# Attention with a compressed memory, then a mixture of experts: a new order of the instructions, gates stored apart, memory products in half-height tiles

## The chip, the cores and the metric

The kernel runs on one core of a Trainium2 chip. The metric is the device time of one execution in microseconds (us). Before the change the median of 3 runs is 526.75 us (526.15 to 527.25). Engines are named as in the profile: PE is TensorE (PEld its weight loads), DVE is VectorE, ACT is ScalarE, POOL is GpSimd, SP is SyncE, which starts most transfers.

## The reference, cut to what matters

Four batches with eight heads, 576 tokens and head size 64 go through causal attention. Beside it each query reads a memory, and a sigmoid of beta mixes the two. The mix, 2304 rows of 512, is routed to one of eight experts.

```python
scores = scale * np.matmul(q, k.transpose(0, 1, 3, 2))      # causal, softmax -> a
local = np.matmul(a, v)
q_p = phi(q)                                                # elu(q) + 1
mem_ret  = np.einsum('bhsd,bhde->bhse', q_p, M_prev)
mem_norm = np.einsum('bhsd,bhd->bhs', q_p, z_prev)[..., None] + 1e-06
x = g * (mem_ret / mem_norm) + (1 - g) * local              # [2304, 512]
logits = x @ w_gate; e_idx = np.argmax(logits, axis=1)
gate_w = softmax(logits)[e_idx]; eom = sigmoid(x @ w_output_gate)
for e in range(8):                                          # rows of expert e
    ye = np.maximum(x[mask] @ w1[e], 0) @ w2[e]
    out[mask] = gate_w[mask, None] * eom[mask, e, None] * ye
```

## The kernel before, in words

The kernel has three stages.

**Attention.** Work goes by pairs of heads, 16 pairs, four per batch. Per pair the scores are computed in query tiles of 128 rows (the last has 64), each fp32 operand split in a rounded part `hi` (C, ACT or DVE) and a rest `lo` (R, POOL). A score tile is masked and its row minimum taken on DVE (M, L555 and L523), turned to weights by ACT (E, L560 and L532), transposed on PE (T, L572 and L541), copied from PSUM by ACT or DVE (V, L419), and multiplied with the values (P, L607; O copies the result). `phi` of the queries is made by POOL, ACT and DVE (F0, F1, F2; L440, L444, L447). When a batch is done, per query tile the memory product (ME, L658), its norm and scaling (N1, N2), the local part turned back (PV, Y) and the sum (XD) follow, and the rows are written to a table `xs` in DRAM (OUT). The routing of a batch (RT, L225 to L239) finds the best expert of each row, RK ranks the rows by matmuls, Tgate and Tpos compute gate value and position on DVE, and SEL (L305, POOL) makes a selection matrix. For the last batch ME is followed by PL, YL, TL, XL and OL, in halves of heads. GO (L275) writes the gate values of a batch into column 512 of `xs`, whose rows are 513 wide.

The order of all this is not left to a scheduler. `ORDER` is a list of some 1150 job names in the file; the jobs are emitted in that order, and each engine runs its own in that order. A suffix (`:ACT`, `:DVE`) says which engine takes a job that two can do. The numbers in the `job(...)` calls (cost, due time, what is taken and used, `mode`, `port`) fed the planner that wrote the list; at run time they do nothing.

**Bridge.** After the list, the last batch is routed (`route`, `rank`, `tail_rank`), and slots of 128 rows are formed: `hit` matrices against the selection matrices give by matmuls (L977) the row number of each place in each slot. `warm(n)` issues n matmuls that nothing reads. Then the first rows are gathered from `xs` by indices (L1033, POOL).

**Experts.** 23 slots of 128 rows go through two matmuls each (L1083), weights split in `whi` and `wlo` as they arrive, and the scaled result is scattered to the output. The scale is the gate value, the 513th column of the gathered row.

The memory product before takes the two heads of a pair in one matmul over all 128 partitions against a block-diagonal matrix of 162 columns, half of them zeros:

```python
for hf in range(2):
    me = psm.tile([P, 324], F32, name=f"me{m}_{hf}", tag="m")
    for pp in range(2):
        T.matmul(me[:r, 162 * pp:162 * pp + 162], t["phi"][2 * hf + pp][:, qz], t["mz"][:, 2 * hf + pp, :], start=True, stop=True)
```

Of the kernel before, what the change touches and what calls it, by code (L numbers as in the profile page):

```python
# [49 lines left out]
SS2_1 F21 M2_0_0 M2_1_0 E2_0_0 F03 E2_1_0 C3:ACT T1_2_1 M2_0_1 V1_2_1:DVE T1_2_0 V1_2_0:DVE P0_256_1 F22 O0_256:ACT F13 M2_1_1 P1_0_0 T1_4 V1_4_0:DVE  # L50
R3 V1_4_1:DVE load4 SS1_3 E2_0_1 load5 M1_3_0 M1_3_1 E2_1_1 SS2_2 T2_0 T2_1 F04 C4:ACT V2_0:ACT MW1 load_v3 E1_3_1 M2_2_0 E2_2_0 gates E1_3_0 V2_1:DVE
SS2_4 T1_3_1 T2_2_0 M2_2_1 V2_2_0:ACT M2_4_0 TS1_0 SS2_3 V1_3_1:DVE M2_4_1 E2_2_1 O1_0:ACT T1_3_0 F05 T2_2_1 M2_3_1 M2_3_0 E2_4 R4 SS3_1 V1_3_0:ACT
E2_3_1 gates2 V2_2_1:DVE E2_3_0 SS3_2 M3_0_0 MC1 P1_256_0 F23 M3_0_1 M3_1_0 T2_3_1 F14 E3_0_0 T2_3_0 P1_256_1 V2_3_0:ACT E3_0_1 O1_256:ACT E3_1_0
V2_3_1:DVE C5:DVE T2_4 M3_1_1 V2_4_0:ACT ME0_0 T3_0 E3_1_1 M3_2_0 F15 V2_4_1:ACT SS3_4 TS1_1 V3_0:ACT M3_2_1 N10_0 SS4_1 TS2_0 T3_1 E3_2_0 N20_0 ME0_1
M3_4_0 R5 M4_0_0 M3_4_1 E3_2_1 M4_1_1 M4_1_0 V3_1:ACT E3_4 N10_1 T3_2_0 TS2_1 load6 M4_0_1 G0_0 T3_2_1 E4_1_1 E4_0_1 V3_2_0:ACT V3_2_1:DVE E4_0_0
SS3_3 N20_1 E4_1_0 SS4_2 F24 M3_3_0 T3_4 P2_256_0 E3_3_0 P2_0_0 V3_4_0:ACT P2_256_1 V3_4_1:ACT O2_256:ACT load_v4 T4_0 M3_3_1 C6:DVE O2_0:DVE TS3_1
T4_1 F25 V4_0:DVE M4_2_1 E3_3_1 ME0_4 M4_2_0 T3_3_0 V4_1:ACT N10_4 N20_4 E4_2_1 SS4_4 V3_3_0:ACT T4_2_1 V4_2_1:ACT E4_2_0 M4_4_0 T3_3_1 ME0_3 T4_2_0
# [1210 lines left out]
```

## Time and profile before

| What | us |
|---|---|
| median of 3 runs | 526.75 |
| profiled execution, device time | 526.39 |
| its span, first to last instruction | 524.4 |
| attention, to about 208.5 | 208.5 |
| bridge, to the first expert matmul | 17.5 |
| experts, to the end | 298.4 |
| PE busy, share of the span | 503.0, 96% |
| DVE, ACT, POOL busy | 340.9, 279.1, 291.1 |

The profiled execution lies 0.36 us below the median, and its device time 2.0 us above its span. A busy PE includes matmuls that wait in the pipeline: durations of single matmuls overlap, so the spacing of their starts is what they cost. PEclk 1.00 is the full clock (2.4 GHz), 0.50 half of it.

### The profile page before, as it was taken

To read this page: it belongs to the slowest core of one execution; us is meant where nothing else is said; L and a number is where in the kernel's file an instruction comes from. 1 tells how busy PE (TensorE), PEld (TensorE's weight loads), DVE (VectorE), ACT (ScalarE), POOL (GpSimd) and SP (SyncE) were. 2 spreads that over 40 slices of the span, in tenths; PEclk is the share of its full clock that TensorE was granted. 3 is DMA by queue.
4 is the path that set the end of the run, shared out by engine and by line. 5 is a ranking of instruction groups with operands and counts; after the bars stand their busy time and mean duration, and the time that the engine had idled before them with its cause. 6 is when DMAs were issued, how large, how long until landed. Compare 5 with 4: busy or idle time off the path is not lost.

```text
span 524.4 us, 10513 instructions
## 1 busy us (share of the span) xinstructions
PE 503.0 (96%) x3238; PEld 402.2 (77%) x3238; DVE 340.9 (65%) x821; ACT 279.1 (53%) x643; POOL 291.1 (56%) x264
## 2 busy tenths in 40 slices
PE   8999999999899999688999999999999999999994
PEld 4788778787777887366888888888888888888884
DVE  5998899999689988659898289500073891025600
ACT  5997788696677864353444333333444433343341
POOL 8882584676355223743577657644455675445342
PEclk9999999999699999889999999999999999999998
DMA  7632155263202513396777367511153675115000
GB/s 247 218 133 101 52 166 160 79 190 100 85 26 77 133 57 91 63 326 228 213 242 225 130 191 216 189 40 48 53 147 114 202 221 160 40 44 158 8 3 27
DMA packets 29079, 68.22 MB, mean 130 GB/s; under 512 B 6176, under 2 KB 6688, under 8 KB 29026
## 3 DMA queue, kind: packets, MB, share of 16 engines
q1 hardware_dynamic: 25186, 56.63, 35.3%
q0 software_dynamic: 3696, 10.77, 5.9%
q8 instruction: 32, 0.52, 0.4%
q14 instruction: 21, 0.17, 0.1%
q10 hardware_dynamic: 144, 0.13, 0.1%
HBM read 58.06 MB, written 10.76 MB: 131 GB/s over the span
## 4 chain that ended last, share of the span: by engine, by line
PE 84%; DVE 8%; POOL 3%; issue 3%; ACT 1%; POOLq 0%; DVEq 0%; ACTq 0%
PE h L1083 23%; PE py L1083 22%; PE pt L572 7%; PE po L607 7%; PE s L497 6%; PE me L658 4%; PE hp L1106 3%; PE sd L484 2%; DVE wlo L944 2%; PE px L1052 2%; PE pt L541 2%; PE pv L721 1%; POOL selp L305 1%; DVE st L555 1%; PE pl L824 1%
## 5 line engine op out<-in xcount | busy, mean ns | idle before, releaser
L941 DVE CAST whi<-raw 128x1024 fp32r<-128x1024 f32 x56 | 56.2, 1004 | 119.4 <-ACTq L1090 109.2
L1111 POOL TENSOR_TENSOR hl<-hT,hh 128x512 fp32r<-128x512 f32 x46 | 68.4, 1507 | 87.4 <-ACT hh L1110 87.4
L944 DVE TENSOR_TENSOR wlo<-raw,whi 128x1024 fp32r<-128x1024 f32 x63 | 95.0, 1508 | 4.0 <-ACT whi L941 1.1
L1083 PE MATMUL py<-whi,hh 128*128 (+1 forms) x192 | 77.8, 405 | 1.6 <-DVEq L947 1.6
L560 ACT ACTIVATE st<-st,nm 128x384 f32<-128x384 f32 (+3 forms) x128 | 71.2, 558 | 14.2 <-DVE nm L555 13.7
L1083 PE MATMUL py<-wlo,hh 128*128 (+1 forms) x192 | 74.2, 386 | 0.0
L1083 PE MATMUL py<-whi,hl 128*128 (+1 forms) x192 | 73.9, 385 | 0.0
L1083 PE MATMUL h<-whi,xh 128*128 (+1 forms) x184 | 73.9, 401 | 0.0
L1083 PE MATMUL h<-wlo,xh 128*128 (+1 forms) x184 | 73.0, 397 | 0.0
L1083 PE MATMUL h<-whi,xl 128*128 (+1 forms) x184 | 72.7, 395 | 0.0
L555 DVE CUSTOM_DVE_ANT_0 st<-s,mask 128x128 f32<-128x128 f32 (+3 forms) x128 | 57.9, 483 | 8.4 <-PE s L497 5.3
L1096 ACT ACTIVATE h<-h 128x1024 f32<-128x1024 f32 x23 | 23.6, 1026 | 73.4 <-PE h L1083 73.4
L392 POOL TENSOR_TENSOR lo<-qk,hi 128x1216 fp32r<-128x1216 f32 x15 | 43.1, 2870 | 27.7 <-ACT hi L388 21.3
L1110 ACT CAST hh<-hp 128x512 fp32r<-128x512 f32 x46 | 27.5, 598 | 48.7 <-PE py L1083 48.7
L419 ACT COPY PT<-pt 128x512 f32<-128x512 f32 (+2 forms) x84 | 42.1, 516 | 17.9 <-PE pt L572 14.5
L572 PE MATMUL pt<-ident,st 128*128 128x128 f32 x320 | 47.9, 281 | 3.2 <-ACT PT L419 2.4
L1060 POOL TENSOR_TENSOR xl<-x,xh 128x512 fp32r<-128x512 f32 x22 | 32.4, 1472 | 33.3 <-ACT x L1059 30.1
L1109 ACT COPY hT<-hp 128x512 f32<-128x512 f32 x46 | 27.2, 590 | 42.5 <-PE hp L1106 42.5
L607 PE MATMUL po<-PT,v 128*64 128x320 f32 (+4 forms) x480 | 47.8, 348 | 0.5 <-DVE oT L419 0.4
L572 PEld LDWEIGHTS pt<-ident,st 128*128 128x128 f32 x320 | 36.7, 143 | 9.7 <-ACT PT L419 4.1
L607 PEld LDWEIGHTS po<-PT,v 128*64 128x64 f32 x480 | 30.0, 137 | 18.4 <-issue 3.2
L1083 PEld LDWEIGHTS py<-whi,hh 128*128 128x128 f32 x192 | 36.2, 188 | 8.3 <-DVEq L947 2.2
(199 smaller groups left out, 998.6 us busy)
## 6 DMA issues: line engine op xcount, KB each, us to landing
raw<-in_w SPq DMA_DIRECT2D x64, 512.0 KB, 4.1
...
```

Of the source, the lines that this page charges most:

```text
L392: G.tensor_tensor(c["lo"][:, TQ:], c["raw"][:, TQ:], f32(c["hi"])[:, TQ:], op=ALU.subtract)
L419: (A.copy if e == "ACT" else V.tensor_copy)(dst(), src())
L497: T.matmul(c()["ss", q][j], l[r, lc], m[r, KC:KC + w], start=(a == 0), stop=(a == 2))
L555: V.tensor_tensor_reduce(st[:, :w], c()["ss", qt][j], mask[:, 512 - w:512], -SCALE, 3.0e38, ALU.add, ALU.min, negm()[:, i:i + 1])
L560: A.activation(st, st, AF.Exp, bias=c()["negm"][:, i:i + 1], scale=-1.0, accum_out=sums()[:, qt, 2 * p + j:2 * p + j + 1])
L572: T.transpose(pt[:, (m * k1 + i) * P:(m * k1 + i + 1) * P], st[:, i * P:(i + 1) * P], ident)
L607: T.matmul(po[64 * j:64 * j + 64, qs - q0:q1 - q0], vt[:, k, 64 * j:64 * j + 64], PT[:, j, k, qs:q1], start=(k == 0), stop=(k == kn - 1))
L941: join((A.copy if eng is A else eng.tensor_copy)(whi[:, e % 2, c, :], raws[e, c]))
L944: join(eng.tensor_tensor(wlo[:, e % 2, c, :], raws.pop((e, c)), f32(whi[:, e % 2, c, :]), op=ALU.subtract))
L1060: G.tensor_tensor(xl, x32, f32(xh), op=ALU.subtract)
L1083: i = T.matmul(o[n % nh], l[:, z], m[:, n * 512 + part.start:n * 512 + part.stop], start=(c == 0 and k == 0 and n < nh), stop=(c == 3 and ...
L1111: G.tensor_tensor(hl[:, z], hT[:, z], f32(hh)[:, z], op=ALU.subtract)
```

## The change

- `ORDER` is written anew for all engines. The jobs are the same but for those below; their order, and for V, O, LC and C the engine, differ. The first line of the list, as an example:

```diff
-first1 load2 SS0_1 M0_0_0 E0_0_0 M0_0_1 M0_1_1 E0_0_1 E0_1_1 first3 first2 M0_1_0 E0_1_0 F00 F01 SS0_3 SS0_2 M0_3_1 load_v2 T0_0 T0_1 M0_3_0 V0_0:DVE
+load2 SS0_1 first1 first2 M0_0_0 E0_0_0 M0_1_1 M0_1_0 M0_0_1 first3 E0_1_1 SS0_3 E0_0_1 M0_3_1 E0_1_0 C1:ACT M0_3_0 F00 SS0_2 T0_0 T0_1 SS0_4 E0_3_1
```

- Memory products: each head is a matmul of its own over 64 partitions and 81 columns, the two heads of a pair in the upper and the lower half of the array.

```diff
-            for hf in range(2):
-                me = psm.tile([P, 324], F32, name=f"me{m}_{hf}", tag="m")
-                for pp in range(2):
-                    T.matmul(me[:r, 162 * pp:162 * pp + 162], t["phi"][2 * hf + pp][:, qz], t["mz"][:, 2 * hf + pp, :], start=True, stop=True)
-                mes.append(me[:r].rearrange("p (h c) -> p h c", c=81))
+            me = [psm.tile([P, 324], F32, name=f"me{m}_{j}", tag="m") for j in range(2)]
+            for p in range(NP):
+                for j in range(2):
+                    z = slice(64 * j, 64 * j + 64)
+                    T.matmul(me[j][:, 81 * p:81 * p + 81], t["phi"][p][z, qz], t["mz"][z, p, 81 * j:81 * j + 81], start=True, stop=True)
+            mes.extend(x[:r].rearrange("p (h c) -> p h c", c=81) for x in me)
```

- Gates: the 128x5 gate values of a batch are transposed on PE (GP), copied from PSUM (GS, on DVE, on ACT for the last batch) into a buffer of which there is one, and written as 5 rows of 512 bytes to a table `gd` of their own (GO). `xs` rows are 512 wide. The expert stage gathers the gates of a slot with an indirect transfer of its own.

```diff
         def gate7():
-            SY.dma_start(xs[row(b, 0):row(b, NQ), DM:XW].rearrange("(t p) c -> p (t c)", p=P), t["og"])
+            t["gp"] = fin.get("pw", psm).tile([P, 512], F32, name=f"gp{b}", tag="m")
+            T.transpose(t["gp"][:NQ, :P], t["og"], ident)
+
+        def gate8():
+            t["gs"] = sm.tile([P, P], F32, name=f"gs{b}", tag="gs", bufs=1)
+            (A.copy if b == B - 1 else V.tensor_copy)(t["gs"][:NQ], t["gp"][:NQ, :P])
+
+        def gate9():
+            SY.dma_start(gd[row(b, 0):row(b, NQ)].rearrange("(t p) c -> t (p c)", p=P), t["gs"][:NQ])
...
+        job(f"GP{b}", "PE", 109, due + DUE["TG"], gate7, after=[before], takes=[("m", f"gp{b}")], uses=[("rb", b)], mode="F")
+        job(f"GS{b}", "DVE", 160, due + DUE["TG"], gate8, after=[f"GP{b}"] + ([f"GO{b - 1}"] if b else []), takes=[("gs", b)], uses=[("m", f"gp{b}")])
+        job(f"GO{b}", "SP", 400, due + DUE["TG"], gate9, after=[f"GS{b}"] + ([f"GO{b - 1}"] if b else []), uses=[("gs", b)], size=10)
...
+    def gather_gate(s):
+        g = st[s]["g"] = mk.tile([P, 1], F32, name=f"g{s}", tag="g", bufs=4)
+        G.indirect_dma_start(out=g, out_offset=None, in_=gd[:NT + 1], in_offset=bass.IndirectOffsetOnAxis(ap=rowi[:, s:s + 1], axis=0))
+
     def gather(s):
-        xr = mk.tile([P, XW], F32, name=f"xr{s}", tag="xr", bufs=4)
+        xr = mk.tile([P, DM], F32, name=f"xr{s}", tag="xr", bufs=4)
         G.indirect_dma_start(out=xr, out_offset=None, in_=xs[:NT + 1], in_offset=bass.IndirectOffsetOnAxis(ap=rowi[:, s:s + 1], axis=0))
         st[s] = {"x": xr, "ring": s < NMAIN}
+        if s > 2:
+            gather_gate(s)
...
-        A.activation(y, py, AF.Copy, scale=st[s]["x"][:, DM:DM + 1])
+        A.activation(y, py, AF.Copy, scale=st[s]["g"])
...
     low(0, 2)
     ready()
+    for s in range(3):
+        gather_gate(s)
```

- Bridge: the second `warm(11)` becomes `warm(22)`, and `warm` and GP take PSUM from a pool of their own there.

```diff
+    fin["pw"] = rx.enter_context(tc.tile_pool(name="pw", bufs=2, space=PSUM))
     warm(8)
...
-    warm(11)
+    warm(22)
```

Three places of the new order follow. The first is PE at the first memory product of batch 0 (`me0_0`; `pt` are transposes of weights, `sd` scores of the 64-row tile, `s` scores). Before:

```order
L541 MATMUL pt2_4_669<-ident_70,st2_4_567 128x128 x4
L543 MATMUL pte2_4_674<-ident_70,st2_4_567 64x128
L658 MATMUL me0_0_0_681<-mz0_184,phi0_223 128x162
L658 MATMUL me0_0_0_681<-mz0_184,phi1_225 128x162
L658 MATMUL me0_0_1_684<-mz0_184,phi2_397 128x162
L658 MATMUL me0_0_1_684<-mz0_184,phi3_448 128x162
L572 MATMUL pt3_0_0_687<-ident_70,st3_0_0_628 128x128
L572 MATMUL pt3_0_0_687<-ident_70,st3_0_1_639 128x128
```

And now:

```order
L508 MATMUL s3_2_0_670<-hi3_472 128x384
L508 MATMUL s3_2_1_671<-hi3_472 128x384
L670 MATMUL me0_0_0_680<-mz0_185,phi0_239 128x81
L670 MATMUL me0_0_1_681<-mz0_185,phi0_239 128x81
L670 MATMUL me0_0_0_680<-mz0_185,phi1_300 128x81
L670 MATMUL me0_0_1_681<-mz0_185,phi1_300 128x81
L670 MATMUL me0_0_0_680<-mz0_185,phi2_307 128x81
L670 MATMUL me0_0_1_681<-mz0_185,phi2_307 128x81
L670 MATMUL me0_0_0_680<-mz0_185,phi3_475 128x81
L670 MATMUL me0_0_1_681<-mz0_185,phi3_475 128x81
L495 MATMUL sd3_4_0_693<-lo3_473,hi3_472 128x288
L495 MATMUL sd3_4_0_693<-hi3_472,lo3_473 128x288
```

Four matmuls of 162 columns became eight of 81, with the two heads of a pair in turn. This product now stands behind row-tiled scores `s`, which read 64 partitions each as well; before it stood among matmuls over the whole array. Over the list, PE passes between layouts of its array (whole, two row halves, column tiles) 109 times now and 91 times before, counted by the jobs' modes.

The second is POOL in batch 1, around the rest of pair 13 (`lo13`; `selp` is a SEL of batch 0, `xd` an XD, `sums` copies of row sums). Before:

```order
L458 COPY sums2_1579<-sumd9_2018 64x1
L729 TENSOR_TENSOR xd1_4_2082<-x1_4_1442,y1_4_1983 64x512
L305 TENSOR_SCALAR selp_78<-pidx_74,pcol_76,tokv_73 128x128 x2
L392 TENSOR_TENSOR lo13_2085<-qk13_1563,hi13_2084 128x1216
L392 TENSOR_TENSOR lo14_2168<-qk14_2002,hi14_2167 128x1216
L458 COPY sums2_1579<-sumd10_2218 64x1
```

And now:

```order
L741 TENSOR_TENSOR xd1_4_2036<-x1_4_1451,y1_4_2019 64x512
L469 COPY sums2_1621<-sumd9_2095 64x1
L403 TENSOR_TENSOR lo13_2080<-qk13_1614,hi13_2079 128x1216
L469 COPY sums2_1621<-sumd8_1899 64x1
L469 COPY sums2_1621<-sumd10_2207 64x1
L316 TENSOR_SCALAR selp_79<-pidx_75,pcol_77,tokv_74 128x128 x2
```

The two SEL now stand behind `lo13`, and `lo14` no longer follows it. `lo14` now stands, behind a row sum of batch 3 (`sums3`) and another SEL:

```order
L469 COPY sums3_2476<-sumd12_2565 64x1
L316 TENSOR_SCALAR selp_79<-pidx_75,pcol_77,tokv_74 128x128
L403 TENSOR_TENSOR lo14_2396<-qk14_2082,hi14_2395 128x1216
L665 MEMSET lg3_2771 128x80
L403 TENSOR_TENSOR lo15_2803<-qk15_1810,hi15_2802 128x1216
L741 TENSOR_TENSOR xd2_2_2810<-x2_2_2496,y2_2_2706 128x512
```

There it is 17 rows of POOL later than before, next to `lo15`.

The third is DVE at the end of the list, from the last product of the last batch (`yl2_1`, job YLl2_1) to the routing of that batch (`mx3`). Before:

```order
L833 TENSOR_TENSOR yl2_1_3255<-pl2_1_3252,rr3_2896 128x320
L836 TENSOR_REDUCE lg3_2730<-yl3_1_3249 128x16
L836 TENSOR_REDUCE lg3_2730<-yl2_1_3255 128x16
L280 TENSOR_TENSOR pos2_3268<-rk2_3258,oha_77 128x40
L283 TENSOR_REDUCE ps2_3269<-pos2_3268 128x5
L286 TENSOR_SCALAR ohe_86<-ps2_3269 128x5
L289 TENSOR_TENSOR pcol_76<-ps2_3269,ohe_86 128x5
L811 CAST cntb_83<-cnt_82 128x8
L225 TENSOR_REDUCE mx3_3302<-lg3_2730 128x5
```

Now, its first seven rows and its last seven:

```order
L847 TENSOR_TENSOR yl2_1_3314<-pl2_1_3303,rr3_3032 128x320
L226 TENSOR_REDUCE mx2_3317<-lg2_1880 128x5
L230 TENSOR_TENSOR dl2_3319<-lg2_1880,mx2_3317 128x40
L234 SCALAR_TENSOR_TENSOR wt2_3321<-dl2_3319,edesc_80 128x40
L237 TENSOR_REDUCE mx2_3317<-wt2_3321 128x5
L240 SCALAR_TENSOR_TENSOR oha_78<-mx2_3317,wt2_3321 128x40
L281 COPY gs0_3325<-gp0_3312 5x128
```

```order
L298 TENSOR_TENSOR pcol_77<-ps2_3344,ohe_87 128x5
L825 CAST cntb_84<-cnt_83 128x8
L850 TENSOR_REDUCE lg3_2771<-yl3_1_3309 128x16
L281 COPY gs1_3365<-gp1_3340 5x128
L281 COPY gs2_3371<-gp2_3361 5x128
L850 TENSOR_REDUCE lg3_2771<-yl2_1_3314 128x16
L226 TENSOR_REDUCE mx3_3398<-lg3_2771 128x5
```

Between these two pieces stand eleven rows with the gates, counts and positions of batch 2. The routing of batch 2 (`mx2` to `oha`) and its gates moved here from the middle of batch 3, 130 rows earlier. The copies `gs1` and `gs2` write the one buffer that the transfers of `gs0` and `gs1` read, so each waits for the transfer before it to land; the sum `lg3` behind `gs2`, and with it `mx3`, stands behind them on DVE.

## Rows read from the trace of the kernel before

**Rows 1.** The page's chain that ended last, shares of the span by engine.

```profile
PE 84%; DVE 8%; POOL 3%; issue 3%; ACT 1%; POOLq 0%; DVEq 0%; ACTq 0%
```

**Rows 2.** Windows; columns: stretch, us, busy of PE/PEld/DVE/ACT/POOL, PEclk, DMA share, GB/s.

```profile
208.50:226.00 17.50, 11.40 (x88) 5.50 (x87) 10.09 (x53) 4.70 (x8) 12.84 (x13) 0.87 0.49 112
...
248.80:524.40 275.60, 268.08 (x1304) 219.86 (x1302) 130.27 (x103) 103.67 (x172) 150.79 (x107) 1.00 0.41 127
```

**Rows 3.** Timeline in batch 1; start, us, engine, line, out<-in, count, idle before.

```profile
124.64 1.56 POOL L305 TENSOR_SCALAR selp<-pidx,pcol,tokv 128x128 f16<-128x128 f16 x2
...
125.40 3.58 DVE L229 TENSOR_TENSOR dl<-lg,mx 128x40 f32<-128x40 f32 x1
126.17 2.75 POOL L392 TENSOR_TENSOR lo<-qk,hi 128x1216 fp32r<-128x1216 f32 x1
...
132.68 1.75 PE L572 MATMUL pt<-ident,st 128*128 128x128 f32 x7 [2.38 <-ACT PT L419]
```

**Rows 4.** Instructions of line 229: duration ns min/median/max, first and last start.

```profile
L229 DVE TENSOR_TENSOR dl<-lg,mx x4: 181/196/3579, 87.1 to 209.8; 128x40 f32<-128x40 f32 x4
```

**Rows 5.** Windows of PE alone, around that stall.

```profile
130.20:132.60 2.40, 0.10 (x1) 1.00 0.60 168
132.60:142.90 10.30, 10.22 (x53) 0.50 0.18 69
```

**Rows 6.** Chain of waits, one of the memory products.

```profile
36.68 1.11 PE me L658 x8
```

**Rows 7.** Timeline of PE's weight loads, at mw and at scores.

```profile
13.36 0.97 PEld L623 LDWEIGHTS mw<-wg,mt 128*128 128x128 f32 x8
14.17 0.72 PEld L572 LDWEIGHTS pt<-ident,st 128*128 128x128 f32 x6
...
39.08 0.19 PEld L497 LDWEIGHTS s<-lo,hi 64*128 64x128 f32 x2
...
39.31 0.19 PEld L497 LDWEIGHTS s<-hi 64*128 64x128 f32 x2
```

**Rows 8.** Waits of PE's weight loads in the attention: us in total, times, longest.

```profile
PEld s L497 <- issue: 4.6, 22, 0.5
...
PEld po L607 <- issue: 3.2, 13, 0.4
...
PEld pt L572 <- issue: 1.4, 4, 0.5
PEld pt L541 <- issue: 1.2, 4, 0.5
```

**Rows 9.** Timeline of DVE in the bridge.

```profile
207.96 0.49 DVE L833 TENSOR_TENSOR yl<-pl,rr 128x320 f32<-128x320 f32 x1
...
209.62 0.19 DVE L225 TENSOR_REDUCE mx<-lg 128x5 f32<-128x40 f32 x1
...
213.44 0.74 DVE L974 TENSOR_TENSOR hit<-sl,sidx 128x80 f16<-128x80 f32 x2
```

**Rows 10.** Timeline of POOL in the bridge.

```profile
209.73 6.01 POOL L305 TENSOR_SCALAR selp<-pidx,pcol,tokv 128x128 f16<-128x128 f16 x6 [0.34 <-DVE pcol L289]
218.74 1.59 POOL L1033 DMA_INDIRECT xr<-xs,rowi  x1 [3.00 <-DVE endi L1010]
```

**Rows 11.** The gates' transfers before, issue to landing.

```profile
DMA to landing us min/median/max: 3.0/4.6/5.5
```

**Rows 12.** Transfers: out<-in, queue, count, median us from issue to landing.

```profile
xr<-xs,rowi POOLq DMA_INDIRECT x23, 5.2
out<-y,outi POOLq DMA_INDIRECT x22, 3.8
```

**Rows 13.** Timeline of PE in the bridge.

```profile
215.80 0.69 PE L977 MATMUL pp<-hit,selp 128*128 128x4 f16 x21 [0.42 <-POOL selp L305]
217.42 4.22 PE L162 MATMUL warm<-ones 128*128 128x512 bf16 x11 [0.93 <-DVE skip L988]
225.02 0.45 PE L1042 MATMUL px_x<-ident,xr 128*128 128x128 f32 x1 [3.38 <-issue]
```

More of the change, by code (lines that the diff above doesn't have):

```diff
@@ L50 @@
[L50 to L57, printed above, removed]
@@ L645, in memory @@
         r = ROWS[qt]
-        qz = slice(TQ + qt * P, TQ + qt * P + P) if qt < NQ - 1 else slice(0, TQ)
+        qz = slice(TQ + qt * P, TQ + qt * P + P) if qt < NQ - 1 else slice(0, P)
         m = f"{b}_{qt}"
-        zs = [slice(4 * hf, 4 * hf + 4) for hf in range(2)]
+        zs = [slice(j, H, 2) for j in range(2)]
         mes = []
@@ L676, in memory @@
         gs = range(NP * b, NP * b + NP)
-        job(f"ME{m}", "PE", 1085, due + DUE["ME"], product, after=[f"F2{g}" for g in gs] + [f"MC{b}"] + ([f"Y{b - 1}_{qt}"] if b else []) + held(due + HOLD["ME"]), takes=[("m", (m, 0)), ("m", (m, 1))], uses=[("phi", g) for g in gs] + [("mz", b)], mode="F")
+        job(f"ME{m}", "PE", 850, due + DUE["ME"], product, after=[f"F2{g}" for g in gs] + [f"MC{b}"] + ([f"Y{b - 1}_{qt}"] if b else []) + held(due + HOLD["ME"]), takes=[("m", (m, 0)), ("m", (m, 1))], uses=[("phi", g) for g in gs] + [("mz", b)], mode="R")
         job(f"N1{m}", "DVE", 460, due + DUE["N1"], norm, after=[f"ME{m}", "gates2"], takes=[("nr", m)], uses=[("m", (m, 0)), ("m", (m, 1))])
@@ L782, in routing @@
         for i, f in enumerate(rs[:5]):
-            job(f"RT{b}_{i}", "DVE", 120, due + DUE["RT"], f, after=[before], port=True)
+            job(f"RT{b}_{i}", "DVE", 120, due + DUE["RT"], f, after=[before], port=True, **(dict(takes=[("rb", b)]) if i == 0 else dict(uses=[("rb", b)])))
             before = f"RT{b}_{i}"
-        job(f"RX{b}", "ACT", 130, due + DUE["RT"], rs[5], after=[f"RT{b}_2", before])
+        job(f"RX{b}", "ACT", 130, due + DUE["RT"], rs[5], after=[f"RT{b}_2", before], uses=[("rb", b)])
@@ L786, in routing @@
         job(f"RK{b}", "PE", 200, due + DUE["RK"], rank, b, after=[before] + ([f"CB{b - 1}"] if b else []), takes=[("m", f"rk{b}")], mode="F")
-        gates, (gate2a, gate7), poss = tails_of(b)
+        gates, (gate2a, gate7, gate8, gate9), poss = tails_of(b)
         before = None
         for f, dep in zip(gates, ([before, f"RT{b}_4"], [f"RX{b}"], [], [], [f"GA{b}"], [])):
-            job(f"T{f.__name__}{b}", "DVE", 115, due + DUE["TG"], f, after=[x for x in dep + [before] if x], port=True)
+            job(f"T{f.__name__}{b}", "DVE", 115, due + DUE["TG"], f, after=[x for x in dep + [before] if x], port=True, uses=[("rb", b)])
@@ L791, in routing @@
             before = f"T{f.__name__}{b}"
-        job(f"GA{b}", "ACT", 120, due + DUE["TG"], gate2a, after=[f"Tgate2{b}"])
-        job(f"GO{b}", "SP", 400, due + DUE["TG"], gate7, after=[before] + ([f"GO{b - 1}"] if b else []), size=200)
+        job(f"GA{b}", "ACT", 120, due + DUE["TG"], gate2a, after=[f"Tgate2{b}"], uses=[("rb", b)])
+        job(f"GP{b}", "PE", 109, due + DUE["TG"], gate7, after=[before], takes=[("m", f"gp{b}")], uses=[("rb", b)], mode="F")
+        job(f"GS{b}", "DVE", 160, due + DUE["TG"], gate8, after=[f"GP{b}"] + ([f"GO{b - 1}"] if b else []), takes=[("gs", b)], uses=[("m", f"gp{b}")])
@@ L810, in routing @@
         job(f"CJ{b}", "DVE", 110, due + DUE["CN"], joined, after=[f"CA{b}"] + ([f"CB{b - 1}"] if b else []), port=True)
-        job(f"CB{b}", "DVE", 200, due + DUE["CN"], lambda: V.tensor_copy(cntb, cnt) and None, after=[f"CJ{b}", f"RK{b}"])
+        job(f"CB{b}", "DVE", 200, due + DUE["CN"], lambda: V.tensor_copy(cntb, cnt) and None, after=[f"CJ{b}", f"RK{b}"], port=True)
     def half(qt, hf, due):
```

139 lines of the change are left out of this document (75 added, 64 removed).

## Prediction

> **What bounds the kernel now.** I began with the chain of waits, by engine: 84% of the span is PE's own work, DVE has 8% and POOL 3% [rows 1]. An edit therefore counts if it shortens PE's stream, lets PE idle, or changes PE's clock. The windows by stage came next. From 248.80 to the end PE is busy 268.08 of 275.60 us at a granted clock of 1.00, so the expert stage is a fixed block whose start alone can move. The bridge is the loose part: PE busy 11.40 of 17.50 us at a clock of 0.87, POOL 12.84 [rows 2].
>
> In the attention I looked for stretches in which PE lost time. The largest is in batch 1. `dl`, an operation of 128x40 that takes 0.196 us elsewhere, took 3.58 from 125.40 on [rows 3, 4]. POOL ran two SEL and then `lo13` (2.75 us from 126.17) in that time; `dl` ended at 128.98 and `lo13` at 128.92 [rows 3]. What stood behind `dl` on DVE came late, and PE started only at 132.68, idle 2.38 us until ACT's copies [rows 3]. After that idle the granted clock was 0.50 for 10.30 us [rows 5], work worth 5.15 at 1.00. The loss is 2.4 + 5.1 = 7.5 us.
>
> That is what the page SBUF — State Buffer of the Trainium skill, section "SBUF: two separate sides", describes: VectorE and GpSimd share a pair of ports, whichever holds it keeps it for its whole instruction, and the other fully blocks. The trace agrees, by the 0.06 us between the two ends above.
>
> **The change part by part**, against the profiled execution's 526.39 us (span 524.4 and 2.0 around it), which is 0.36 below the median of 526.75.
>
> *Memory products.* There are 20, each 8 passes over the array in 1.10 us [rows 6]; all are on PE's path, so a gain in them counts in full. Now each is 16 passes of 81 columns, two heads in turn in the two row halves. The nearest rows: eight full-height loads in a row take 14.17 − 13.36 = 0.81 us, 0.101 each; loads of score matmuls in row halves come in pairs, and two pairs take 39.31 − 39.08 = 0.23, 0.115 a pair [rows 7]. Eight pairs would take 0.81 by the first spacing and 0.92 by the second. I take 0.87, the middle: 20 × (0.87 − 1.10) = −4.6, bounds −5.8 and −3.6. (That pairs do not overlap is a rival below.)
>
> The page TensorE: Matmul & The Clock Gate, section "LDWEIGHTS (loading the stationary operand)", speaks against this part: a load's time goes by its columns and not by its rows, so that twice as many loads of half height cost twice as much. The same page, section "The mechanism", lets loads of different row groups overlap, and the pairs above agree with that.
>
> *Layout changes of the array.* 109 instead of 91. Before a change PE waits for nothing that shows, and the rows that say so sum to 4.6 + 3.2 + 1.4 + 1.2 = 10.4 us in the attention [rows 8]; over 91 changes that is 0.11 each, and 18 more cost 2.0. Bounds: 0, if the new ones fall where PE waits anyway, and 18 × 4.6/22 = 3.8, if all cost what those before scores do [rows 8]. I take 2.0, since some changes go into scores and some out of them.
>
> *The stall.* The two SEL now stand behind `lo13`, and `dl1` stands next to `cntb`. What is late next is the ordinary neighbour on DVE. I credit 5.0 of the 7.5: a rewritten order of 1150 jobs has other places where DVE or ACT comes late, and a third of this loss may come back in smaller ones. Bounds: −7.5, and 0 with a stall as large elsewhere (a rival).
>
> *The tail on DVE.* Before, the last `yl` started at 207.96 and `mx3` at 209.62 [rows 9], with two sums and five small operations between. Now the routing of batch 2, its gates and positions, and `gs0`, `gs1`, `gs2` stand there too: about 20 more operations, less the position work that stood there already. DVE's small operations in the bridge start 0.1 to 0.25 us apart, and I work the extra out as 2.6 us. Then the one buffer of the gates: `gs1` waits until the transfer of `gs0` has landed, `gs2` until that of `gs1` has. A transfer of gates landed after 3.0 us at the fastest and 4.6 in the median [rows 11]. I take 3.0, because the new ones have 5 rows of 512 bytes in place of 640 single values. Behind `gs0` stand some 1.8 us of work, so `gs1` waits 1.2; `gs2` follows `gs1` directly and waits all 3.0. Together `mx3` is late by 2.6 + 1.2 + 3.0 = 6.8. Queued behind them on DVE are the last sum, `mx3` and the whole route to the `hit` matrices. Before, these were ready at 213.44 + 0.74 = 214.18, while the last group of `pp` matmuls started at 215.80, held by POOL's six SEL [rows 9, 10, 13]: 1.6 us of slack. Most of those SEL are of batch 2, whose positions now come from the same stretch, so POOL is late as well, and I give back 1.0 only. The end moves by 6.8 − 1.0 = +5.8. Bounds: +1.5, if no transfer is waited for (2.6 − 1.1), and +8.9, if each lands after 4.6 (2.8 + 4.6 in waits, 2.6 of work, 1.1 of slack).
>
> The page DMA: Bandwidth & Descriptors, section "Anatomy of one DMA — SWDGE (gpsimd) path", gives about 2.0 us of fixed cost per transfer. By it, as an estimate, the waits would be 0.2 and 2.0 and the end +3.8; no row here shows a landing under 3.0 for these.
>
> *Rows gathered by index.* `xr` has 2052 bytes a row now and lands after 5.2 us in the median; the scatter of 2048 after 3.8 [rows 12]. Only the first is on the path, between 218.74 and `px` at 225.02 [rows 10, 13]. I take half of the 1.4 between them, −0.7; bounds −1.4 and 0.
>
> *Warm.* Eleven took 4.22 us, 0.38 each, and PE then stood idle 3.38 until the first rows [rows 13]. Their first part ran at half clock; at full clock eleven more fit into that idle, and at 0.38 each they would outlast it by 0.84. What they can give is a full clock at the start of the experts; the bridge's 11.40 us of PE at 0.87 hold 11.40 x 0.13 = 1.5 us of lost clock in all [rows 2]. Bounds −1.5 and +0.8; I take 0, since PE idles in either case.
>
> *The rest at nothing.* The gates' gathers for slots 0 to 2 lie in POOL's free stretch before the second slot, those of later slots in its share of idle in the experts. Three transposes of gates are 0.1 us each on PE.
>
> Sum: −4.6 + 2.0 − 5.0 + 5.8 − 0.7 = −2.5, and 526.39 − 2.5 = **523.9 us**, 2.85 below the median.
>
> **The rivals.**
>
> R1, *the tail wait is hidden.* If the transfers of `gs0` and `gs1` land before DVE gets to the next copy, because DVE is late for another reason (it waits for PE's `pl` products there), the tail costs +1.5 and not +5.8: 523.9 − 4.3 = 519.6. Against it: `gs2` stands directly behind `gs1`, with no work between.
>
> R2, *a new stall takes the place of the old one* (the other side). `lo14` is 17 rows of POOL later than before and next to `lo15`, each about 2.75 us [rows 3]. Two paths lead to a stall: PE's scores of pair 14 come to need `lo14` before it is done, or a DVE operation on SBUF runs beside the two and waits as `dl` did. It decides once PE has idled about as long as the 2.38 us after which the clock fell to half [rows 3, 5]. A stall of the old size then costs 7.5 where the sum kept 2.5 for all of them: 523.9 + 5.0 = 528.9. For it: this is how the loss before came about, and batch 3 has the densest work on DVE. Against it: the scores of pair 14 stand late in PE's list too.
>
> R3, *the loads of a pair do not overlap.* Sixteen at 0.101 are 1.62 a product, +10.4 over 20 instead of −4.6: 523.9 + 15 = 538.9. Against it are the score pairs [rows 7].
>
> R4, *the products gain nothing* because a change of layout stands before each and eats it (18 × 0.21 = 3.8, products at 0.92): −3.6 + 3.8 in place of −2.6, 526.7. This lies inside the forecast's own range, and its chance, 0.08, is part of the forecast's.
>
> **How the numbers follow.** A measurement of this kernel can tell about 0.2%, 1.05 us, from no change: faster is below 525.7, slower above 527.8. Forecast 0.48 (own range 520.5 to 527), R1 0.17, R2 0.26, R3 0.05, anything else 0.04. Of the forecast's 0.48, 0.34 lie below 525.7, 0.10 within and 0.04 above. R1 gives 0.16 faster and 0.01 the same; R2 0.02 faster, 0.05 the same and 0.19 slower; R3 0.05 slower; the rest 0.02 on each side. Sums: 0.54 faster, 0.16 the same, 0.30 slower. The range goes from 518.5, about one us below R1, to 531.5, some 2.6 above R2; R3 and the ends of all bounds at once are left out.
>
> **What the profile after would show.** Products: `me` in the chain at 0.81 to 0.92 us each; near 1.6 is R3. Layout changes: "issue" before `s`, `po` and `pt` sums to some 12.4. Stall: all four `dl` near 0.2 us and no slice of batch 1 with a halved clock; one elsewhere, above all before scores of pairs 14 and 15, is R2. Tail: DVE idle before `gs1` and `gs2`, about 1.2 and 3.0, and `mx3` some 6.8 after its old distance of 1.66 from the last `yl`; no idle there is R1. Gather: from the first `xr` to `px` 5.6 in place of 6.3. Whatever these steps give, the stretch from the first expert matmul to the end should stay within 1 us. The prediction is wrong if that block changes, or if the attention changes by much more than −7.6 us, its three terms here.

## The result and the profile after

The changed kernel takes 522.2 us (median of 6 runs, 520.29 to 523.46), the kernel before 526.68 (6 runs, 525.62 to 527.86). The ratio is 0.9912, 95% interval 0.9890 to 0.9934: faster by 4.6 us, interval 3.5 to 5.8. The forecast was 2.85 us, with a range that holds the measured time. The mechanisms are told apart stage by stage, since two of them were missed and stand against each other.

Times between fixed points of the two profiled executions (spans 524.4 and 520.3 us):

| from, to | before | after | change | forecast |
|---|---|---|---|---|
| start, last `yl` product on DVE | 207.96 | 200.61 | −7.35 | −7.6 |
| last `yl`, `mx3` | 1.66 | 5.77 | +4.11 | +6.8 |
| `mx3`, first gather `xr` | 9.12 | 6.27 | −2.85 | −1.0 |
| `xr`, first `px` on PE | 6.28 | 6.39 | +0.11 | −0.7 |
| `px`, first expert matmul | 0.92 | 0.70 | −0.22 | 0 |
| first expert matmul, last scatter | 291.78 | 291.15 | −0.63 | 0 |
| last scatter, end of span | 6.68 | 9.41 | +2.73 | 0 |
| sum | | | −4.10 | −2.5 |

The −2.85 up to the first gather has two parts, which meet at `rowi`, the indices that the gather reads. From `mx3` to the first `rowi` it is 6.39 before and 5.12 after (−1.27), from there to the gather 2.73 and 1.15 (−1.58). Before, then after:

```profile
216.01 0.16 DVE L982 TENSOR_SCALAR rowi<-pp 128x4 int32<-128x4 f32 x1 [1.55 <-PE pp L977]
```

```profile
211.50 0.16 DVE L997 TENSOR_SCALAR rowi<-pp 128x4 int32<-128x4 f32 x1
```

First the chain of waits of the changed kernel, on its page. It answers [rows 1]: PE still has 84%, DVE 5% in place of 8%.

```profile
PE 84%; DVE 5%; POOL 3%; DMA 2%; issue 2%; ACT 2%; POOLq 0%; SPq 0%; DVEq 0%; ACTq 0%
```

The windows of its bridge and its expert stage, columns as in [rows 2]. POOL is busy 169.80 us in the second, where it was 150.79: the gathers of gates. PE's 268.01 us there are unchanged.

```profile
201.10:219.74 18.64, 13.65 (x108) 6.51 (x108) 12.94 (x70) 5.25 (x12) 12.19 (x14) 0.91 0.35 116
242.04:520.30 278.26, 268.01 (x1304) 220.04 (x1303) 133.54 (x103) 103.63 (x172) 169.80 (x126) 0.99 0.41 126
```

The four `dl` of the changed kernel (duration in ns, minimum, median, maximum), for [rows 4]. The one of 3.58 us is gone.

```profile
L230 DVE TENSOR_TENSOR dl<-lg,mx x4: 191/200/422, 75.5 to 206.6; 128x40 f32<-128x40 f32 x4
```

A smaller stall stands elsewhere. The timeline at 80 to 84 us in batch 0 and, behind it, PE's windows (us, PE busy, granted clock, DMA share, GB/s):

```profile
79.37 2.81 POOL L403 TENSOR_TENSOR lo<-qk,hi 128x1216 fp32r<-128x1216 f32 x1
...
82.11 0.18 POOL L665 MEMSET lg<- 128x80 f32 x1
...
82.32 0.37 DVE L686 TENSOR_REDUCE lg<-x 128x16 f32<-128x128 f32 x1 [1.93 <-POOL lg L665]
82.60 0.68 DVE L737 TENSOR_TENSOR y<-pv,rr 128x512 f32<-128x512 f32 x1
...
83.34 1.12 PE L670 MATMUL me<-mz,phi 64*128 64x81 f32 x16 [1.09 <-DVE y L737]
```

```profile
80.00:84.40 4.40, 3.31 (x36) 1.00 0.30 71
84.40:88.40 4.00, 3.68 (x26) 0.57 0.44 172
```

VectorE waited 1.93 us for POOL to clear `lg`, which stood behind a `lo` of 2.81; PE was idle 1.09 + 0.32 us and then ran at a clock of 0.57 for 4 us, 1.7 us lost. Together about 3.1.

The memory products, in PE's weight loads, for [rows 6, 7]. Sixteen loads take 0.89 us to the next load where scores in row halves follow (7 of the 20 products), 1.05 or more where work over the whole array does (13).

```profile
50.74 0.97 PEld L670 LDWEIGHTS me<-mz,phi 64*128 64x128 f32 x16 [0.17 <-DVE nm L534]
51.63 0.19 PEld L508 LDWEIGHTS s<-lo,hi 64*128 64x128 f32 x2
...
53.71 0.97 PEld L670 LDWEIGHTS me<-mz,phi 64*128 64x128 f32 x16
54.76 0.20 PEld L552 LDWEIGHTS pt<-ident,st 128*128 128x128 f32 x2
```

The waits of weight loads for nothing that shows, for [rows 8]: 3.6 + 2.4 + 1.3 + 0.9 = 8.2 us, where the same four rows of before sum to 10.4.

```profile
PEld s L508 <- issue: 3.6, 17, 0.5
...
PEld po L618 <- issue: 2.4, 14, 0.2
...
PEld pt L583 <- issue: 1.3, 4, 0.5
...
PEld pt L552 <- issue: 0.9, 3, 0.5
```

DVE, then SP, at the end of the list, for [rows 9]. The copy at 202.48 is `gs0`, then `gs1` without a wait, then `gs2` with 1.32. SP issued the transfer of `gs1` at 204.58, and it had landed by 205.87: 1.3 us, not 3.0.

```profile
200.61 0.49 DVE L847 TENSOR_TENSOR yl<-pl,rr 128x320 f32<-128x320 f32 x1
...
202.48 0.27 DVE L281 COPY gs<-gp 5x128 f32<-5x128 f32 x1
...
204.28 0.27 DVE L281 COPY gs<-gp 5x128 f32<-5x128 f32 x1
205.87 0.28 DVE L281 COPY gs<-gp 5x128 f32<-5x128 f32 x1 [1.32 <-DMA gd<-gs]
...
206.38 0.20 DVE L226 TENSOR_REDUCE mx<-lg 128x5 f32<-128x40 f32 x1
```

```profile
204.58 0.27 SPq L284 DMA_DIRECT2D gd<-gs  x1
```

POOL and PE in the bridge, for [rows 10, 13]. The `pp` matmuls no longer wait for POOL, the first gather follows 0.67 us behind their end, and PE's idle before `px` is 2.30.

```profile
209.18 0.97 POOL L316 TENSOR_SCALAR selp<-pidx,pcol,tokv 128x128 f16<-128x128 f16 x1 [1.09 <-DVE og L273]
212.65 1.23 POOL L1052 DMA_INDIRECT xr<-xs,rowi  x1 [2.50 <-DVE need L1018]
```

```profile
210.82 1.16 PE L992 MATMUL pp<-hit,selp 128*128 128x4 f16 x40
211.83 4.91 PE L163 MATMUL warm<-ones 128*128 128x512 bf16 x22
219.04 0.30 PE L1063 MATMUL px_x<-ident,xr 128*128 128x128 f32 x1 [2.30 <-issue]
```

The program's last records are not counted as busy, and the views put the end down to SP's wait for PE. The trace's own records of POOL there name what lasts (start us, ns): before, 47 transfers by POOL; after, 70.

```
before  518.50  1149  GpSimd INC_SWDGE_SEM
before  519.68  3917  GpSimd DRAIN
after   512.04  1608  GpSimd INC_SWDGE_SEM
after   513.68  5796  GpSimd DRAIN
```

These two last 5.07 us before and 7.40 after. That is 2.3 of the 2.73 us that the end grew.

### The profile page after: what moved, and what is told of

It reads as the page before. It is cut to its first block, busy times and chain, and to the rows that moved or that the text cites. A ratio compares the mean times of both kernels' runs of the same rounds, so it can differ in the third digit from the quotient of the medians.

```text
span 520.3 us, 10907 instructions
## 1 busy us (share of the span) xinstructions
PE 498.1 (96%) x3413; PEld 397.1 (76%) x3413; DVE 339.0 (65%) x826; ACT 278.8 (54%) x642; POOL 311.9 (60%) x287
## 4 chain that ended last, share of the span: by engine, by line
PE 84%; DVE 5%; POOL 3%; DMA 2%; issue 2%; ACT 2%; POOLq 0%; SPq 0%; DVEq 0%; ACTq 0%
PE h L1104 23%; PE py L1104 22%; PE po L618 8%; PE pt L583 7%; PE s L508 6%; PE hp L1127 4%; PE me L670 3%; PE sd L495 2%; DVE wlo L958 2%; PE px L1073 2%; PE pt L552 2%; DMA raw<-in_w 1%; PE warm L163 1%; PE pv L733 1%; PE pl L838 1%
## 5 line engine op out<-in xcount | busy, mean ns | idle before, releaser
L958 DVE TENSOR_TENSOR wlo<-raw,whi 128x1024 fp32r<-128x1024 f32 x63 | 98.7, 1567 | 3.2 <-issue 0.9
L571 ACT ACTIVATE st<-st,nm 128x128 f32<-128x128 f32 (+3 forms) x128 | 71.1, 558 | 7.1 <-DVE nm L566 6.9
L430 ACT COPY PT<-pt 128x512 f32<-128x512 f32 (+2 forms) x80 | 40.4, 519 | 16.0 <-PE pt L583 12.5
L1104 PEld LDWEIGHTS py<-wlo,hh 128*128 128x128 f32 x192 | 36.1, 188 | 8.1
L1104 PEld LDWEIGHTS h<-whi,xl 128*128 128x128 f32 x184 | 34.6, 188 | 8.7 <-POOL xl L1081 0.4
```

What stands on the lines that cost most here:

```text
L430: (A.copy if e == "ACT" else V.tensor_copy)(dst(), src())
L571: A.activation(st, st, AF.Exp, bias=c()["negm"][:, i:i + 1], scale=-1.0, accum_out=sums()[:, qt, 2 * p + j:2 * p + j + 1])
L958: join(eng.tensor_tensor(wlo[:, e % 2, c, :], raws.pop((e, c)), f32(whi[:, e % 2, c, :]), op=ALU.subtract))
L1104: i = T.matmul(o[n % nh], l[:, z], m[:, n * 512 + part.start:n * 512 + part.stop], start=(c == 0 and k == 0 and n < nh), stop=(c == 3 and ...
```

## The experiments

Each was timed beside the kernel before on its own chip; ratios are to that, and medians of different runs can come from different chips, so the ratios decide. One us is 0.0019 of a ratio. Six of the profiled runs lose some 1.5 us to a half clock within the first 16 us, which neither of the two main profiles shows; so stages are compared by their length, not by when they end.

**Memory products whole again** (changed kernel). The four matmuls of 162 columns are back, with `zs` and `qz` to match:

```diff
-            for p in range(NP):
-                for j in range(2):
-                    T.matmul(me[j][:, 81 * p:81 * p + 81], t["phi"][p][z, qz], t["mz"][z, p, 81 * j:81 * j + 81], start=True, stop=True)
+            for hf in range(2):
+                for pp in range(2):
+                    T.matmul(me[:r, 162 * pp:162 * pp + 162], t["phi"][2 * hf + pp][:, qz], t["mz"][:, 2 * hf + pp, :], start=True, stop=True)
```

> The changed kernel with its memory products as they were (four matmuls of 162 columns over the whole array, 1.08 us each between loads), the order kept. Theory A (the terms of the sum: products -4.6, layout changes +2.0): the attention ends 2.6 us later than in the changed kernel, ratio to before about 0.996. Theory B (what the product gives depends on its neighbours alone: 0.88 us between row-tiled neighbours, 0.17 more for each neighbour over the whole array; the changed order has 2 products between two of the first kind, 13 between one of each, 5 between two of the second): 2 x 0.53 + 13 x 0.19 - 5 x 0.15 = 2.8 us later. Theory C (the products give nothing, the new order all): 0 within 0.5. A and B are told apart by the next run, not by this one.

Ratio 0.9981 (0.9959 to 1.0003), against 0.9912: 3.6 us slower than the changed kernel by the ratios, 2.9 by the medians (525.08 and 522.2), both with over 1 us of uncertainty. So C falls. In its trace the distance from the first load of one product to that of the next is longer than in the changed kernel by 0.17 us on average for a product behind scores in row halves and ahead of whole-array work (7 of them), by 0.46 for one behind whole-array work and ahead of scores (3), by 0.02 between two of whole-array work (4; stretches with a stall left out). The two between scores on both sides give +0.21 and −0.22, which fits no such rule. The load row and what follows shows the largest case: 1.31 to the next load, where the changed kernel has 0.89.

```profile
51.35 1.13 PEld L669 LDWEIGHTS me<-mz,phi 128*128 128x128 f32 x8
52.66 0.19 PEld L508 LDWEIGHTS s<-lo,hi 64*128 64x128 f32 x2 [0.17 <-issue]
```

The pair of traces also differs in the clock, twice and in opposite directions. In this run PE did not fall to half clock in the stall near 84 us (1.00 in the window below, 0.86 in the changed kernel), which saves it some 1.3 us. Its first expert matmuls did run at half clock, 0.43 apart, and the stretch from the first of them to the last scatter is 292.35 us in place of 291.15. The attention is 2.15 us longer, so the products themselves are worth some 3.4.

```profile
80.00:92.00 12.00, 11.11 (x93) 1.00 0.24 83
```

**Memory products alone** (kernel before, the reverse edit, order untouched).

> The kernel before with nothing changed but the memory products (row halves, 81 columns). In its order 19 of the 20 stand between work over the whole array. Theory A (4.6 us less for the products, 38 more layout changes at 0.11 = 4.2 more): 0.4 us less, ratio about 0.999. Theory B (each such product takes 0.88 + 2 x 0.17 = 1.22 in place of 1.08): 19 x 0.14 = 2.7 us more, ratio about 1.005, and loads of a product and what follows start 1.05 apart with another 0.17 ahead of the product. Theory C (products give nothing): 0.

Ratio 1.0005 (0.9986 to 1.0023): within 1.2 us of nothing. A's −0.4 fits, B's +2.7 does not. The row shows why it is no gain: the product is shorter by 0.03 and waits 0.17 first.

```profile
52.47 0.97 PEld L659 LDWEIGHTS me<-mz,phi 64*128 64x128 f32 x16 [0.17 <-issue]
53.52 0.31 PEld L572 LDWEIGHTS pt<-ident,st 128*128 128x128 f32 x3
```

B would make that a loss of 0.14 each, yet four products from the first on take 18.22 us (before 18.14), five later ones 32.77 (32.82). Why the 0.17 does not show in these sums stays open. In the profiled execution the half clock behind the old stall lasts 13.7 us, where it lasted 10.2 before, though PE's idle ahead of it is 2.14 in place of 2.38; so the ratio alone could hide a gain. The two sums lie outside that stretch and show none. In this order the products gain nothing.

**`dl` early** (kernel before).

```diff
-... LA1 E9_4 Tpos40 OUT1_2 E10_0_1 TS9_0 O8_0:DVE RT1_0 SEL0_4 SEL0_3 ...
+... LA1 RT1_0 RT1_1 E9_4 Tpos40 OUT1_2 E10_0_1 TS9_0 O8_0:DVE SEL0_4 SEL0_3 ...
...
-RT1_1 E10_2_1 F113 ...
+E10_2_1 F113 ...
```

> The kernel before with two small operations of batch 1's routing (mx and dl) put ahead of the positions of batch 0 on VectorE, so that dl runs before POOL has selection matrices to make. If dl's 3.58 us beside POOL's selections and lo13 made the stall: dl about 0.2 us, no idle of 2.38 before the transposes, no stretch at half clock near 133 to 143, and the attention 5 to 7.5 us shorter, ratio 0.986 to 0.990. If any VectorE operation on two SBUF operands waits there (phi behind lo13), the stall comes back smaller: 2 to 4 us shorter. If the stall has another cause: no change.

Ratio 0.9985 (0.9966 to 1.0004), not told apart from no change. `dl` takes 0.20 us, and `phi`, the next operation on two SBUF operands, takes 3.78 in its place (0.75 of it its own work, as the `phi` after it shows), beside the second SEL and `lo13`. PE's idle is 2.25, and half clock follows it again, for 6.8 us in place of 10.2. The second theory is right that the wait moves on, and too hopeful of the gain.

```profile
122.12 0.20 DVE L229 TENSOR_TENSOR dl<-lg,mx 128x40 f32<-128x40 f32 x1
...
127.72 3.78 DVE L447 SCALAR_TENSOR_TENSOR phi<-qk,phi 128x576 f32<-128x576 f32 x1
...
134.06 0.98 PE L572 MATMUL pt<-ident,st 128*128 128x128 f32 x7 [2.25 <-ACT PT L419]
```

**The selections later** (kernel before; the two SEL in front of `lo13`).

```diff
-SS10_4 SEL0_2 E10_3_1 F215 V10_3_0:ACT Tgate11 SEL0_0 V10_2_1:ACT N12_1 R13 ...
+SS10_4 E10_3_1 F215 V10_3_0:ACT Tgate11 V10_2_1:ACT N12_1 R13 ...
...
-R14 E11_1_1 Tpos41 ...
+R14 SEL0_2 SEL0_0 E11_1_1 Tpos41 ...
```

> The kernel before with the two selections of batch 0 that stood before lo13 on POOL moved behind lo14. If VectorE's dl waits for whatever POOL runs, as the port rule says: lo13 starts 1.5 us earlier, dl ends with it and lasts some 2.0 us in place of 3.58, what follows on VectorE comes 1.6 us earlier, PE's idle before the transposes falls from 2.4 to about 0.8 and the clock stays at 1.00: up to 6.7 us of the 7.5, ratio 0.987 to 0.990. If the clock falls all the same after the shorter idle: 1.6 us, ratio 0.997.

Ratio 0.9963 (0.9938 to 0.9987): 1.9 us faster, 0.7 to 3.3, where up to 6.7 was expected. In the profiled execution `dl` takes 2.04, as said, PE's idle falls to 0.85, and the clock stays at 1.00. The same windows as in [rows 5]:

```profile
126.06 2.77 POOL L392 TENSOR_TENSOR lo<-qk,hi 128x1216 fp32r<-128x1216 f32 x1
...
126.85 2.04 DVE L229 TENSOR_TENSOR dl<-lg,mx 128x40 f32<-128x40 f32 x1
...
132.60 0.98 PE L572 MATMUL pt<-ident,st 128*128 128x128 f32 x7 [0.85 <-ACT PT L419]
```

```profile
130.20:132.60 2.40, 1.55 (x13) 1.00 0.63 194
132.60:142.90 10.30, 8.86 (x77) 1.00 0.17 63
```

The half clock is gone with the longer idle, but PE idles 1.44 us behind a late `cntb` in the second window: a stall removed leaves a smaller one. `cntb` is a cast with one SBUF operand; it takes 0.17 us elsewhere and 2.24 here, beside `lo14` on POOL, so two SBUF operands are not the only case. The idle and the clock came out as the first theory says, the time did not: its ratio of 0.997 for a clock that falls all the same is the nearer one. The mean granted clock of the twelve executions goes from 0.976 to 0.991 (0.988 in the profiled one), so the others may have fallen to half clock where this one did not. No trace shows them, and the missing gain stays open.

**`lg` cleared by VectorE** (changed kernel).

```diff
-                G.memset(t["lg"], 0.0)
+                V.memset(t["lg"], 0.0)
```

> The changed kernel with the clearing of lg (once a batch) on VectorE in place of POOL. In the changed kernel VectorE idles 1.93 us at 80.4 for that clearing, which stands behind lo of 2.81 us on POOL, and PE then idles 1.09 + 0.32 us and runs at half clock for 3.4 us: some 3.1 us in all. If that clearing is the cause: no such idle, the clock 1.00 in 80 to 88, the attention 2 to 3.1 us shorter, ratio to before 0.985 to 0.987. If VectorE would be late there anyway: under 0.5 us.

Ratio 0.9891 (0.9851 to 0.9930), median 519.59. The windows of the stall are full, at full clock, and the last `yl` starts at 197.75, 2.86 us earlier: in the profiled executions the new stall cost that. The ratio lies above the expected 0.985 to 0.987 and, with its interval, is not told apart from the changed kernel's 0.9912.

```profile
80.00:84.40 4.40, 4.40 (x46) 1.00 0.29 85
84.40:88.40 4.00, 4.00 (x46) 1.00 0.40 156
```

**`gs2` on ScalarE** (changed kernel).

```diff
-            (A.copy if b == B - 1 else V.tensor_copy)(t["gs"][:NQ], t["gp"][:NQ, :P])
+            (A.copy if b >= B - 2 else V.tensor_copy)(t["gs"][:NQ], t["gp"][:NQ, :P])
```

> The changed kernel with gs2, the copy of batch 2's gates that waited 1.32 us on VectorE for a transfer, made by ScalarE, which idles 3.68 us there. If that wait sets the end of the bridge: the routing's mx3 1.6 us earlier behind the last yl (4.2 in place of 5.77), and the first px as much earlier, ratio to before about 0.988 against 0.991 of the changed kernel. If something else holds the first rows (POOL's selection matrices, the transfers): px at most 0.5 us earlier.

Ratio 0.9904 (0.9878 to 0.9929), not told apart from the changed kernel. `mx3` comes 4.16 us behind the last `yl`, 1.6 earlier as said; `px` comes 0.7 earlier. The rest went into PE's queue: the matmuls of rank and `pp` stand behind bursts of warming matmuls, and DVE waits 0.59 us for `pp`.

```profile
212.53 0.16 DVE L997 TENSOR_SCALAR rowi<-pp 128x4 int32<-128x4 f32 x1 [0.59 <-PE pp L992]
```

**Gates in the rows again** (changed kernel; `xs` 513 wide, GP and GS empty, no gather of gates).

```diff
-            SY.dma_start(gd[row(b, 0):row(b, NQ)].rearrange("(t p) c -> t (p c)", p=P), t["gs"][:NQ])
+            SY.dma_start(xs[row(b, 0):row(b, NQ), DM:XW].rearrange("(t p) c -> p (t c)", p=P), t["og"])
```

> The changed kernel with the gates as before: written value by value into a 513th column of the rows, no copies gs, no transfers g; order, products and warm as changed. Theory A (23 transfers fewer on POOL make the drain at the program's end shorter): from the start of the last scatter to the end of the span 6.7 us in place of 9.4. Theory B (the end depends on something else of the change, such as code loading): 9.4 stays. Bridge: mx3 2.1 us earlier behind the last yl (no wait of 1.32, no copies), but the first rows wait for the slow transfer of gates, as before the change (xr 9.1 us behind mx3, in place of 6.3): px 0.5 to 1 later behind the last yl. Sum by A: 2 us less than the changed kernel, ratio 0.987; by B 0.5 to 1 more, 0.993.

Ratio 0.9963 (0.9939 to 0.9986): 2.7 us slower than the changed kernel by the ratios, 1.7 by the medians. The end is 6.75 us long again, with POOL's two records at 1136 and 3917 ns, so A holds for the end, though not for its sum of 0.987. The first gather comes 10.72 us behind `mx3`, in place of 6.27. Of these 4.45 us 0.73 lie ahead of the first `rowi`, where DVE waited 0.71 for an earlier transfer of gates, and 3.72 between `rowi`, ready at 212.63, and the gather. SP had issued the last transfer of gates into the rows at 212.53.

```profile
212.53 0.37 SPq L282 DMA_DIRECT2D xs<-og  x1
```

```profile
217.34 1.23 POOL L1044 DMA_INDIRECT xr<-xs,rowi  x1 [6.21 <-DVE wlo L954]
```

The view puts the wait down to `wlo`. The trace's own records of POOL's waits and of the landings settle it (us): the gather follows its wait for the last transfer of gates, here and in the kernel before.

| | last transfer issued | its last landing | POOL's wait for it ends | gather starts |
|---|---|---|---|---|
| before | 212.76 | 217.46 | 217.48 | 218.74 |
| gates in the rows | 212.54 | 216.06 | 216.08 | 217.34 |

In the three other runs on the kernel before, too, the gather starts 1.28 us behind that landing. In the changed kernel the wait that ends last is the one for the indices. In the profiled executions it is 2.1 us more from the last `yl` to `px`, 0.7 more from there to the last scatter and 2.7 less at the end, which nearly cancel; the stages do not account for all that the ratio shows.

**Each gather of gates twice** (changed kernel).

```diff
-        G.indirect_dma_start(out=g, out_offset=None, in_=gd[:NT + 1], in_offset=bass.IndirectOffsetOnAxis(ap=rowi[:, s:s + 1], axis=0))
+        for o in (mk.tile([P, 1], F32, name=f"g2_{s}", tag="g2", bufs=4), g):
+            G.indirect_dma_start(out=o, out_offset=None, in_=gd[:NT + 1], in_offset=bass.IndirectOffsetOnAxis(ap=rowi[:, s:s + 1], axis=0))
```

> The changed kernel with every gather of gates issued twice, the first into a tile that nothing reads: 23 more transfers on POOL. Theory A (the drain at the end grows with the number of such transfers, 0.12 us each): from the last scatter's start to the end of the span 12.1 us in place of 9.4, ratio about 0.996. Theory B: 9.4 as before, and only POOL is busier by some 1 us a slot, which it has to spare: ratio 0.991.

Ratio 1.0102 (1.0057 to 1.0146). POOL's two records at the end last 2.05 + 7.67 = 9.72 us with 93 transfers: 5.07, 7.40, 9.72 for 47, 70 and 93, 0.101 us a transfer. A holds for these records; the whole stretch from the last scatter is 13.06 us, where 12.1 was expected. Neither theory foresaw the rest: the stretch from the first expert matmul to the last scatter grew by 8 us, and PE waits 6.9 us in it for POOL's `xl`.

```profile
PE h L1105 <- POOL xl L1082: 6.9, 4, 4.8
```

**Eleven warming matmuls** (changed kernel, `warm(22)` back to `warm(11)`).

> The changed kernel with eleven warming matmuls before the first rows, as before. If they are worth what the clock shows: the first expert matmuls start 0.43 apart in place of 0.23 for some six of them, the stretch from the first of them to the last scatter 0.6 to 1.2 us longer, ratio 0.992 to 0.993. If PE's idle of 2 to 3 us before the first rows lowers the clock in either case: no difference.

Ratio 0.9951 (0.9928 to 0.9974), 2.1 us slower than the changed kernel by the ratios, 1.1 by the medians. In the profiled executions the stretch from `px` to the last scatter shows 0.7 of it. Four of the first expert matmuls start 0.43 apart, where some six were expected:

```profile
220.64 0.63 PE L1104 MATMUL h<-whi,xl 128*128 128x512 f32 x1
221.07 0.63 PE L1104 MATMUL h<-wlo,xh 128*128 128x512 f32 x1
```

**All together** (changed kernel with `lg` on VectorE, `gs2` on ScalarE, and the bursts before rank and `pp` cut).

```diff
-    warm(8)
+    warm(5)
...
-            warm(11)
+            warm(8)
```

> The changed kernel with the clearing of lg on VectorE (worth 3.1 us by its run), gs2 copied by ScalarE (mx3 1.6 us earlier by its run, of which 0.7 reached the end, since the matmuls of rank and pp then stood behind the warming ones), and the two earlier bursts of warming cut from 8 to 5 and from 11 to 8, so that nothing waits behind them. If these waits add: px 1.5 us earlier behind the last yl than in the changed kernel (16.9 in place of 18.4), the attention 3 us shorter, in all 4.5 us less than the changed kernel, ratio to before about 0.983. If the shorter bursts lower the clock before the first rows: 0.987 to 0.989, as with the clearing alone.

Ratio 0.9873 (0.9840 to 0.9906), median 519.2: faster than the kernel before, and not told apart from the clearing alone. Against the changed kernel it is 2.1 us less by the ratios, with about as much uncertainty, and 3.0 by the medians. `px` comes 16.65 us behind the last `yl`, 1.8 earlier than in the changed kernel, but matmuls at the start of the experts run at half clock again, eight of them 0.43 apart:

```profile
217.61 0.63 PE L1104 MATMUL h<-whi,xl 128*128 128x512 f32 x1
218.03 0.63 PE L1104 MATMUL h<-wlo,xh 128*128 128x512 f32 x1
```

## Why the prediction was right, and where its terms were off

The direction and the likeliest case were right. The attention is right to 0.25 us. Behind it three terms came out lower than forecast (the tail by 2.7, the first gather by 1.0, warm and the start of the experts by 0.85) and one was missed on the other side (the end, +2.7), so that the sum is nearer than its terms. That is luck: nothing ties the tail, the gather and the clock to the end of the program, and without the missed end the forecast change of −2.5 would have stood against −6.8. One sign of being wrong that the prediction named did come: the stretch from the first expert matmul to the end was to stay within 1 us and grew by 2.10 (−0.63 + 2.73).

- *Memory products −4.6, layout changes +2.0* (together −2.6). Measured with the products whole: 2.9 us by the medians, 3.6 by the ratios, 3.4 in the attention with the stall's clock set aside. The split was wrong in kind: the runs show no price per product and one per change, but a gain of 0.2 to 0.5 us with scores on one side and none between whole-array work. Only the seven products ahead of row-tiled scores reach the 0.81 to 0.92 that were to be seen, the other 13 take 1.05 or more. The 1.10 before stands as 1.11 in [rows 6], and the loads show 1.08. The rows in front of `s`, `po` and `pt` fell to 8.2 us, where 12.4 were forecast. R3, near 1.6 a product, and R4 did not come.
- *The stall −5.0 of 7.5.* The old stall went, by where POOL's long work stands and not by what became of `dl`: `dl` alone moved gives its wait to `phi`. The 2.5 us kept for "other places where DVE or ACT comes late" is the stall at 80 to 88 us, 2.86 by its removal. R2 thus happened in small, in batch 0, by a clearing on POOL and not by `lo14` and `lo15`, at 2.9 of its 7.5 us. It took less idle than the 2.38 us of R2: half clock followed 1.09 + 0.32 us here, while none followed the 1.44 us behind `cntb` (the selections later). That this is about what the forecast had kept is luck too, since no row gave the size of what would come back. Nor is 7.5 a fixed price: behind much the same idle the half clock lasted 6.8, 10.2 and 13.7 us (`dl` early, before, products alone).
- *The tail +6.8 up to `mx3`.* Measured +4.1. The mis-sized term is the landing: 3.0 us were taken from transfers of 640 single values, and five rows of 512 bytes land in 1.3. So `gs1` waits 0 in place of 1.2 and `gs2` 1.32 in place of 3.0. With single values in the same order, gates in the rows, the last transfer lands after 3.5. The page DMA: Bandwidth & Descriptors of the Trainium skill, section "Anatomy of one DMA — SWDGE (gpsimd) path", gives its 2.0 for transfers that GpSimd issues. It was nearer than my 3.0, but these transfers are issued by SP, so it is no figure for them.
- *1.0 given back, gather −0.7.* The 1.0 was nearly right: up to the first `rowi` the route is 1.27 shorter. A failed step is behind it, where the sum has no term at all: before the change the first gather had to wait until the last gate value had landed in the same rows, and the change takes away 1.58 us there. The row of POOL at 218.74 put the wait down to `endi` [rows 10]; 4.6 us of landing behind the last transfer of gates, issued at 212.76, would have shown it (it landed after 4.7). With gates put back into the rows the wait returns, 3.72 us in that order. What I did price, the width of the gathered row at −0.7, gives nothing: from `xr` to `px` the change is +0.1, and with the wide rows in the changed order it is 5.90 us in place of 6.39.
- *The rest at nothing.* This step failed too, and it is the one behind that sign: 23 more transfers by POOL cost 2.3 us in its records at the program's end. I looked for their cost only where they are issued. There it was hidden, but with less to spare than I said: the doubled gathers made PE wait.
- *Warm 0.* It gives 1.1 us (medians) or 2.1 (ratios, 0.4 to 3.7) by its removal; the profiled executions show 0.7. The bound of −1.5 was drawn from the wrong stretch: the lost clock of the bridge [rows 2] ends where the matmuls that warming can speed up begin. My reason, that PE idles in either case, did not hold for the changed kernel: after an idle of 2.30 us its first expert matmuls run at full clock. With the same 22 and idles of 2.04 and 2.09 us (`gs2` on ScalarE, all together) they run at half clock for a while, and behind 2.04 us with the doubled gathers at full clock, so the length of the idle alone does not decide; what does stays open, and with it how often the 22 help. To the last scatter the stretch of the experts changed by −0.63 only.
